# Weight conversions behind attention, ordered behind the newest split or copy

## The chip, the core and the metric

The kernel runs on one core of a Trainium2 chip: TensorE (PE in the profile, with its weight loads as PEld), VectorE (DVE), ScalarE (ACT), GpSimd (POOL) and SyncE (SP), each with a queue of its own that it works through in order. The metric is device time in microseconds of one execution, the median of the runs. 1 % is 10.4 us here.

## What is computed

Attention with a causal mask and a cumulative bias, then two dense layers with an activation between two matrix products each. Only the first dense layer (`_moe_ref`) lies in the stretch that the change touches; its four matrices are stored as 64-bit floats, which the kernel must turn into 32-bit pairs first.

```python
def _moe_ref(x, w_in, w_out):            # x: 2304 x 512, w_in: 512 x 2048, w_out: 2048 x 512
    h = x @ w_in
    g = h * (1.0 / (1.0 + np.exp(-1.702 * h)))
    return (g @ w_out).astype(np.float32)

def reference(**kwargs):
    ...
    attn_out = _attn_ref(**attn_kwargs)  # 4 batches, 8 heads, 576 positions, 64 wide
    B, H, S, D = attn_out.shape
    x = np.ascontiguousarray(attn_out.transpose(0, 2, 1, 3)).reshape(B * S, H * D)
    x = _moe_ref(x=x, **moe_kwargs)
    return _moe2_ref(x=x, **moe2_kwargs)
```

## The kernel before

**Precision and tiles.** Every operand of a matrix product is kept as a high and a low part, so that each product is three matmuls. A dense layer is cut into 16 columns of d_ff (`f`, 128 wide each); the weights of one `f` are a unit `u` of two halves, `w_in` and `w_out`, each 128 x 512. The tokens are cut into 8 blocks of 288.

**Stages of the first layer.** `mlp1_first` runs `f` = 0 to 4; for the first three batches it runs as filler within attention, for the last batch alone behind it, and each of its blocks ends in copies `st` of the sums (line 613, on ScalarE for odd `d`, on VectorE for even ones). `mlp1_rest` then runs `f` = 5 to 11 over all 8 blocks, and again `f` = 12 to 15. One step of it is `stage1` (12 matmuls into a bank `h`, line 575), `act1` (tanh on ScalarE, a product on VectorE, then the split of the result: the high part `gh` by ScalarE, line 589, the low part `gl` by VectorE, line 592) and `out1` for the step two before it (12 matmuls, line 599). At a block's end VectorE adds the block's sums to those of the pass before (`xp`, line 659), GpSimd's queue stores them and SyncE's queue loads the next block's (line 649). The second dense layer, `mlp2`, follows.

**Conversions.** `convert` (line 495 on) turns one half of raw 64-bit weights into a high and a low part: three ScalarE instructions (lines 500, 502, 508) and, behind attention, five on VectorE (503, 504, 505, 507, 509). Some halves go straight into a unit `u`; others into `park` and from there by GpSimd's queue into DRAM (line 555), to be fetched later. `task` puts a conversion in a queue; `emit` takes the next one, `look_ahead` keeps `LEAD` = 2 loads of raw weights (lines 489, 491, SyncE's queue) ahead of it; the raw tiles have 4 buffers. Behind attention `mlp1_first` emits eight conversions (`EARLY`), and `mlp1_rest` calls `tick` at each step, which by `PACE` = 0.5 emits one at every second step, 40 in all.

**What sets the order.** The program is written in the order above, but a scheduler orders each engine's queue by times that it reckons itself when the program is built; an instruction may stand well ahead of its place in the text when its inputs are reckoned to be there. `issue_after`, through `behind`, binds the instructions that a block of code emits to stand behind a given instruction of the same engine; it adds no wait on another engine. Within attention conversions are already bound in this way behind `self.tail` (the newest exponential and reciprocal); `wide` is false there and true behind it.

Of the kernel before, what the change touches and what calls it, by code (L numbers as in the profile page):

```python
# [15 lines left out]
AF = mybir.ActivationFunctionType  # L16
# [18 lines left out]
HB = S // 2  # L35
# [24 lines left out]
class Fused:  # L60
    def __init__(self, tc, q, k, v, s, w1i, w1o, w2i, w2o, a, b, out):
        self.tc, self.nc = tc, tc.nc
        self.q, self.k, self.v, self.s = q, k, v, s
        self.w = {n: (i.bitcast(I32), o.bitcast(I32)) for n, i, o in ((1, w1i, w1o), (2, w2i, w2o))}
        self.a, self.b, self.out = a, b, out
        self.units = {}
        self.acts = []


    def consts(self, pool):  # L70
# [456 lines left out]
    def emit(self, n):  # L527
        for _ in range(min(n, len(self.queue))):
            src, work = self.queue.pop(0)
            work(self.ahead.pop(0) if self.ahead else self.load_raw(src))  # L530
            self.look_ahead()

    def look_ahead(self):
# [49 lines left out]
    def act1(self, pool, h, w, bufs):  # L583
        nc = self.nc
        g = pool.tile([P, HB], F32, name="g", tag="g", bufs=2)
        nc.scalar.activation(g[:, :w], h, AF.Tanh, scale=0.851)  # L586
        nc.vector.scalar_tensor_tensor(g[:, :w], g[:, :w], 1.0, h, ALU.add, ALU.mult)  # L587
        gh = pool.tile([P, HB], F32R, name="gh", tag="gh", bufs=bufs)
        nc.scalar.activation(gh[:, :w], g[:, :w], AF.Copy)  # L589
        gl = pool.tile([P, HB], F32R, name="gl", tag="gl", bufs=bufs)  # L590
        eng = nc.vector if self.wide else nc.gpsimd
        gl_op = eng.tensor_tensor(gl[:, :w], g[:, :w], gh[:, :w].bitcast(F32), ALU.subtract)  # L592
        self.acts.append(gl_op)
        return gh, gl

    def out1(self, acc, u, d, g, first, last):
# [7 lines left out]
    def out1_block(self, pool, blk, gs):  # L604
        nc = self.nc
        for d in range(KD):
            acc = self.bank("a" if self.wide else "M", f"a{blk}_{d}")
            for f in range(F1):
                self.out1(acc[:, :HB], self.units[1, f], d, gs[f], f == 0, f == F1 - 1)
                if f % 2 and f < F1 - 1:  # L610
                    yield 0.74
            st = pool.tile([P, HB], F32, name="st", tag="st", bufs=2)
            (nc.scalar.copy if d % 2 else nc.vector.tensor_copy)(st, acc[:, :HB])
            nc.sync.dma_start(self.x2p[d * P : (d + 1) * P, blk * HB : (blk + 1) * HB], st)
            yield 0.37

# [328 lines left out]
```

## Time and profile before

| | us |
|---|---|
| median of 3 runs | 1044.78 |
| the runs | 1044.45, 1044.78, 1049.55 |
| the profiled execution | 1049.78 |
| its span, first to last instruction | 1048.0 |

The profiled execution lies 5.0 us above the median and next to the slowest of the three runs. A slice or window row gives each engine's busy time and, in brackets, its count of instructions in that stretch; PEclk is the granted share of TensorE's full clock; a timeline row gives start, duration, engine, line and, in square brackets, how long the engine stood idle just before and what released it. Attention ends at about 315 us, `mlp1_first` of the last batch at 347.9, `mlp1_rest` at 642.

### The profile page before, as it was taken

To read this page: it belongs to the slowest core of one execution; us is meant where nothing else is said; L and a number is where in the kernel's file an instruction comes from. 1 tells how busy PE (TensorE), PEld (TensorE's weight loads), DVE (VectorE), ACT (ScalarE), POOL (GpSimd) and SP (SyncE) were. 2 spreads that over 40 slices of the span, in tenths; PEclk is the share of its full clock that TensorE was granted. 3 is DMA by queue.
4 is the path that set the end of the run, shared out by engine and by line. 5 is a ranking of instruction groups with operands and counts; after the bars stand their busy time and mean duration, and the time that the engine had idled before them with its cause. 6 is when DMAs were issued, how large, how long until landed. Compare 5 with 4: busy or idle time off the path is not lost.

```text
span 1048.0 us, 19871 instructions
## 1 busy us (share of the span) xinstructions
PE 1015.2 (97%) x7074; PEld 945.2 (90%) x7074; DVE 812.1 (77%) x1874; ACT 721.3 (69%) x1660; POOL 322.7 (31%) x429
## 2 busy tenths in 40 slices
PE   7978999999999999989999999999999999999997
PEld 4767999999999999989999999899899999999996
DVE  6898868766637898885397345898998988989886
ACT  5898879888756765654264235787877777777775
POOL 6357745634320003331111112223222222222222
PEclk9998999999999999999999999999999999999999
DMA  7455356454217658894246537010010100100000
GB/s 180 119 155 147 99 150 192 121 138 101 54 41 278 193 173 287 280 302 150 71 145 206 179 121 259 1 31 31 1 61 1 31 31 1 59 3 1 31 1 31
DMA packets 79596, 116.72 MB, mean 111 GB/s; under 512 B 25697, under 2 KB 63585, under 8 KB 77901
## 3 DMA queue, kind: packets, MB, share of 16 engines
q1 hardware_dynamic: 73128, 95.96, 31.0%
q0 software_dynamic: 6144, 19.19, 5.1%
q8 instruction: 56, 0.92, 0.4%
q14 instruction: 44, 0.35, 0.1%
q10 hardware_dynamic: 224, 0.30, 0.1%
HBM read 75.08 MB, written 32.05 MB: 102 GB/s over the span
## 4 chain that ended last, share of the span: by engine, by line
PE 82%; ACT 4%; issue 4%; DMA 4%; DVE 3%; POOL 2%; SPq 0%; ACTq 0%; POOLq 0%; DVEq 0%
PE h L575 33%; PE a L751 19%; PE a L599 15%; PE s L255 5%; PE O L370 4%; PE tp L344 3%; DMA raw<-in_moe_w_in_dram 2%; POOL wd L555 1%; ACT bt L292 1%; PE idle L79 1%; DMA raw<-in_moe_w_out_dram 1%; PE tk L218 1%; DVE bt L285 1%; ACT kh L180 1%; PE tq L218 1%
## 5 line engine op out<-in xcount | busy, mean ns | idle before, releaser
L575 PE MATMUL h<-x,u 128*128 128x288 f32 x1536 | 231.2, 298 | 7.2 <-DVE g L587 4.2
L599 PE MATMUL a<-gh,u 128*128 128x288 f32 x1024 | 227.1, 297 | 2.2 <-ACT gh L589 2.2
L575 PEld LDWEIGHTS h<-x,u 128*128 128x128 f32 x1536 | 213.6, 189 | 10.6 <-DVE g L587 4.9
L734 POOL TENSOR_TENSOR gl<-u,gh 128x384 fp32r<-128x384 f32 x96 | 105.5, 1099 | 291.4 <-ACT gh L732 255.7
L599 PEld LDWEIGHTS a<-gh,u 128*128 128x128 f32 x1024 | 171.1, 188 | 4.1 <-ACT gh L589 2.6
L575 PE MATMUL h<-y,u 128*128 128x384 f32 x864 | 165.7, 336 | 0.0
L575 PEld LDWEIGHTS h<-y,u 128*128 128x128 f32 x864 | 152.9, 188 | 6.2
L599 PE MATMUL a<-gl,u 128*128 128x288 f32 x512 | 147.7, 295 | 0.8 <-DVE gl L592 0.7
L751 PE MATMUL a<-u,gh 128*128 128x512 f32 x432 | 114.6, 394 | 0.9 <-ACT gh L732 0.9
L304 POOL TENSOR_SCALAR bt<-bt,sm 128x128 f32<-128x128 f32 (+2 forms) x144 | 82.1, 582 | 105.8 <-DVE sm L301 66.4
L660 POOL DMA_DIRECT2D x<-xp x64 | 35.3, 552 | 226.6 <-DVE g L587 95.4
L586 ACT ACTIVATE g<-h 128x288 f32<-128x288 f32 x128 | 51.5, 406 | 75.0 <-PE h L575 67.0
L599 PEld LDWEIGHTS a<-gl,u 128*128 128x128 f32 x512 | 96.4, 188 | 2.3 <-DVE gl L592 1.8
L292 ACT ACTIVATE bt<-bt,mn 128x128 f32<-128x128 f32 (+2 forms) x144 | 83.6, 582 | 18.0 <-DVE mn L285 17.1
L751 PEld LDWEIGHTS a<-u,gh 128*128 128x128 f32 x432 | 80.0, 188 | 14.9 <-ACT gh L732 1.8
L587 DVE SCALAR_TENSOR_TENSOR g<-g,h 128x288 f32<-128x288 f32 x128 | 57.1, 449 | 45.8 <-ACT g L586 45.6
L285 DVE CUSTOM_DVE_ANT_0 bt<-s,mask 128x128 f32<-128x128 f32 (+2 forms) x144 | 69.0, 482 | 26.4 <-PE s L255 22.4
L732 ACT ACTIVATE gh<-u 128x384 fp32r<-128x384 f32 x96 | 50.6, 528 | 55.6 <-DVE u L730 55.4
L717 ACT ACTIVATE y<-h,cf 128x384 f32<-128x384 f32 x96 | 55.5, 579 | 36.7 <-PE h L575 36.7
L255 PE MATMUL s<-k 68*128 68x256 f32 (+2 forms) x192 | 72.1, 380 | 5.5 <-DMA k<-stgA 3.2
L722 DVE SCALAR_TENSOR_TENSOR y<-s,cf,y 128x384 f32<-128x384 f32 x96 | 59.3, 618 | 21.2 <-ACT s L719 19.5
L730 DVE SCALAR_TENSOR_TENSOR u<-y,u 128x384 f32<-128x384 f32 x96 | 73.6, 767 | 1.1
(107 smaller groups left out, 2068.0 us busy)
## 6 DMA issues: line engine op xcount, KB each, us to landing
raw<-in_moe_w_in_dram SPq DMA_DIRECT2D x24, 512.0 KB, 5.2
raw<-in_moe_w_out_dram SPq DMA_DIRECT2D x24, 512.0 KB, 3.8
x<-xp POOLq DMA_DIRECT2D x64, 144.0 KB, 2.8
wd<-park POOLq DMA_DIRECT2D x36, 256.0 KB, 5.0
u<-wd SPq DMA_DIRECT2D x8, 1024.0 KB, 10.4
x2p<-st SPq DMA_DIRECT2D x32, 144.0 KB, 2.4
xp<-x2p SPq DMA_DIRECT2D x32, 144.0 KB, 2.7
xp<-x SPq DMA_DIRECT2D x32, 144.0 KB, 2.7
```

Source lines behind the costliest of these rows:

```text
L255: nc.tensor.matmul(sc[: c1 - c0, :w], lhsT=q[:, c0:c1], rhs=k[:, j0 : j0 + w], start=m == 0, stop=m == 1,)
L285: nc.vector.tensor_tensor_reduce(bt[:, j0 : j0 + w], sc[:, :w], mask, 1.0, 3.0e38 if i == 0 else mn[:, 0:1], ALU.add, ALU.min, mn[:, i : i ...
L292: ex = nc.scalar.activation(bt[:, :n], bt[:, :n], AF.Exp, bias=mn[:, i : i + 1], scale=-1.0, accum_out=sm[:, col : col + 1],)
L304: nc.gpsimd.tensor_scalar(bt[:, :n], bt[:, :n], inv[:, i : i + 1], 1.0, ALU.mult, ALU.mult)
L575: nc.tensor.matmul(ps_tile, lhsT=u[:, wl, kk * P : (kk + 1) * P], rhs=x(xl, kk), start=(n == 0), stop=(n == 3 * KD - 1),)
L587: nc.vector.scalar_tensor_tensor(g[:, :w], g[:, :w], 1.0, h, ALU.add, ALU.mult)
L599: nc.tensor.matmul(acc, lhsT=u[:, wl, d * P : (d + 1) * P], rhs=g[gl], start=(first and i == 0), stop=(last and i == 2),)
L717: nc.scalar.activation(y, h, AF.Abs, scale=cf[:, 4:5])
L722: nc.vector.scalar_tensor_tensor(y, s, cf[:, 7:8], y, ALU.mult, ALU.add)
L730: last = nc.vector.scalar_tensor_tensor(p, y, 2.0, p, ALU.subtract, ALU.mult)
L734: nc.gpsimd.tensor_tensor(gl, p, gh.bitcast(F32), ALU.subtract)
L751: nc.tensor.matmul(accs[m], lhsT=g[gl][:, m * P : (m + 1) * P], rhs=u[:, wl, :], start=(f == 0 and i == 0), stop=(f == NF - 1 and i == 2),)
```

## The change

Three things are recorded where they are issued: the newest `gh` or ScalarE copy `st` under "act", and the newest `gl` or VectorE copy `st` under "dve". When a conversion's turn comes and `wide` is set, its instructions on these two engines are bound behind those. The load of the raw weights stays outside this, and runs two ahead as before. The list `acts`, which nothing read, goes.

```diff
-        self.acts = []
+        self.newest = {}
...
             src, work = self.queue.pop(0)
-            work(self.ahead.pop(0) if self.ahead else self.load_raw(src))
+            staged = self.ahead.pop(0) if self.ahead else self.load_raw(src)
+            with self.behind(self.newest.values() if self.wide else ()):
+                work(staged)
             self.look_ahead()
...
-        nc.scalar.activation(gh[:, :w], g[:, :w], AF.Copy)
+        self.newest["act"] = nc.scalar.activation(gh[:, :w], g[:, :w], AF.Copy)
...
-        self.acts.append(gl_op)
+        self.newest["dve"] = gl_op
...
-            (nc.scalar.copy if d % 2 else nc.vector.tensor_copy)(st, acc[:, :HB])
+            key, copy = ("act", nc.scalar.copy) if d % 2 else ("dve", nc.vector.tensor_copy)
+            self.newest[key] = copy(st, acc[:, :HB])
```

The queues that come of it are equal up to the end of `mlp1_first` and from `mlp2` on; between them all five differ. In the rows below `h2_2_8` is the `h` of block 2, `f` = 8; `raw` and `cvx` are a conversion's tiles, told apart by their last number; a line number behind 527 stands two or three higher after the change.

**ScalarE, block 2 of the first pass of `mlp1_rest`.** Before:

```order
L586 ACTIVATE g_6171<-h2_2_8_6158 128x288
L589 ACTIVATE gh_6134<-g_6131 128x288
L508 ACTIVATE park_5475<-cvx_6520 128x512
L500 ACTIVATE raw_6609<-raw_6609 128x512
L502 ACTIVATE cvx_6773<-raw_6609 128x512
L589 ACTIVATE gh_6174<-g_6171 128x288
L586 ACTIVATE g_6216<-h2_2_9_6203 128x288
L586 ACTIVATE g_6248<-h2_2_10_6235 128x288
L500 ACTIVATE raw_6698<-raw_6698 128x512
L589 ACTIVATE gh_6219<-g_6216 128x288
```

After, the same steps:

```order
L588 ACTIVATE g_6171<-h2_2_8_6158 128x288
L508 ACTIVATE park_5475<-cvx_6105 128x512
L591 ACTIVATE gh_6174<-g_6171 128x288
L500 ACTIVATE raw_6026<-raw_6026 128x512
L502 ACTIVATE cvx_6190<-raw_6026 128x512
L588 ACTIVATE g_6216<-h2_2_9_6203 128x288
L591 ACTIVATE gh_6219<-g_6216 128x288
L508 ACTIVATE park_5475<-cvx_6190 128x512
L588 ACTIVATE g_6248<-h2_2_10_6235 128x288
```

The 25th raw tile (`raw_6609`), whose conversion has its turn at block 4, stood ahead of `gh_6174` of block 2; now the 18th (`raw_6026`) stands there, behind that `gh`, and each split follows its tanh with at most one conversion instruction between them.

**ScalarE, the end of `mlp1_first`** (`a7_1`, `a7_3`: sums of the last block; `raw_5353`: the eighth raw tile). Before:

```order
L613 COPY st_5419<-a7_1_5403 128x288
L500 ACTIVATE raw_5353<-raw_5353 128x512
L502 ACTIVATE cvx_5429<-raw_5353 128x512
L508 ACTIVATE u1_10_5301<-cvx_5302 128x512
L508 ACTIVATE u1_10_5301<-cvx_5344 128x512
L613 COPY st_5466<-a7_3_5450 128x288
L500 ACTIVATE raw_5500<-raw_5500 128x512
```

After:

```order
L616 COPY st_5419<-a7_1_5403 128x288
L500 ACTIVATE raw_5353<-raw_5353 128x512
L502 ACTIVATE cvx_5429<-raw_5353 128x512
L508 ACTIVATE u1_10_5301<-cvx_5302 128x512
L616 COPY st_5466<-a7_3_5450 128x288
L508 ACTIVATE u1_10_5301<-cvx_5344 128x512
L588 ACTIVATE g_5489<-h2_0_5_5476 128x288
```

One of the two line-508 instructions moved behind the last copy; the eighth raw tile still stands ahead of it.

**VectorE, the end of block 6 of the first pass** (`a2_6_5_0` to `_3`: the block's four sums). Before:

```order
L587 SCALAR_TENSOR_TENSOR g_7489<-g_7489,h2_7_5_7476 128x288
L592 TENSOR_TENSOR gl_7494<-g_7489,gh_7492 128x288
L659 TENSOR_TENSOR xp_7315<-a2_6_5_0_7225,xp_7315 128x288
L587 SCALAR_TENSOR_TENSOR g_7536<-g_7536,h2_7_6_7523 128x288
L659 TENSOR_TENSOR xp_7317<-a2_6_5_1_7226,xp_7317 128x288
L659 TENSOR_TENSOR xp_7319<-a2_6_5_2_7227,xp_7319 128x288
L659 TENSOR_TENSOR xp_7321<-a2_6_5_3_7228,xp_7321 128x288
```

After:

```order
L594 TENSOR_TENSOR gl_7494<-g_7489,gh_7492 128x288
L503 TENSOR_SCALAR cvx_7512<-cvx_7512 128x512
L504 TENSOR_SCALAR cvx_7512<-cvx_7512 128x512
L662 TENSOR_TENSOR xp_7315<-a2_6_5_0_7225,xp_7315 128x288
L589 SCALAR_TENSOR_TENSOR g_7536<-g_7536,h2_7_6_7523 128x288
L505 SCALAR_TENSOR_TENSOR cvx_7512<-raw_7366,cvx_7512 128x512
L662 TENSOR_TENSOR xp_7317<-a2_6_5_1_7226,xp_7317 128x288
L662 TENSOR_TENSOR xp_7319<-a2_6_5_2_7227,xp_7319 128x288
L662 TENSOR_TENSOR xp_7321<-a2_6_5_3_7228,xp_7321 128x288
```

No conversion stood near this block's end before; now one lies around and between its four adds.

## Rows read from the trace of the kernel before

**Rows 1.** The page: span, busy times of the engines, granted clock in 40 slices.

```profile
span 1048.0 us, 19871 instructions
PE 1015.2 (97%) x7074; PEld 945.2 (90%) x7074; DVE 812.1 (77%) x1874; ACT 721.3 (69%) x1660; POOL 322.7 (31%) x429
PEclk9998999999999999999999999999999999999999
```

**Rows 2.** Windows by stage, all engines: from, to, length, busy times and counts.

```profile
core 0: us, PE busy (x) PEld busy (x) DVE busy (x) ACT busy (x) POOL busy (x), PEclk, DMA share, GB/s
325.00:350.00 25.00, 22.51 (x168) 22.02 (x166) 20.81 (x46) 17.42 (x36) 0.00 (x0) 1.00 0.76 243
350.00:404.00 54.00, 53.84 (x395) 53.84 (x396) 51.44 (x114) 37.24 (x78) 5.82 (x11) 0.97 0.64 195
404.00:475.00 71.00, 64.20 (x471) 62.34 (x471) 57.01 (x126) 39.45 (x84) 23.40 (x42) 1.00 0.88 288
475.00:525.00 50.00, 50.00 (x380) 50.00 (x379) 21.49 (x51) 17.11 (x40) 6.52 (x12) 1.00 0.34 108
525.00:575.00 50.00, 50.00 (x380) 50.00 (x379) 44.37 (x100) 29.32 (x62) 6.96 (x12) 1.00 0.51 170
```

**Rows 3.** TensorE's waits from 404 to 475: us in total, times, longest.

```profile
PE h L575 <- DVE g L587: 4.2, 3, 1.6
PE a L599 <- ACT gh L589: 2.2, 2, 1.4
```

**Rows 4.** Timeline of ScalarE and TensorE around 414 us.

```profile
413.76 0.65 ACT L500 ACTIVATE raw<-raw 128x512 int32<-128x512 uint32 x1 [3.65 <-DMA raw<-in_moe_w_in_dram]
...
414.87 0.43 ACT L589 ACTIVATE gh<-g 128x288 fp32r<-128x288 f32 x1
...
415.34 0.79 PE L599 MATMUL a<-gh,u 128*128 128x288 f32 x4 [1.43 <-ACT gh L589]
```

**Rows 5.** ScalarE's waits from 404 to 475, the two on raw weights.

```profile
ACT raw L500 <- DMA raw<-in_moe_w_out_dram: 12.6, 7, 4.4
ACT raw L500 <- DMA raw<-in_moe_w_in_dram: 11.6, 6, 3.7
```

**Rows 6.** Line 500's instructions from 350 to 404, 404 to 475, 475 to 642.

```profile
L500 ACT ACTIVATE raw<-raw x15: 666/684/702, 350.0 to 401.6; 128x512 int32<-128x512 uint32 x15
...
L500 ACT ACTIVATE raw<-raw x16: 652/676/702, 407.2 to 474.3; 128x512 int32<-128x512 uint32 x16
...
L500 ACT ACTIVATE raw<-raw x9: 667/683/695, 475.2 to 552.3; 128x512 int32<-128x512 uint32 x9
```

**Rows 7.** Timeline of ScalarE and TensorE where `mlp1_rest` begins.

```profile
346.88 0.67 ACT L500 ACTIVATE raw<-raw 128x512 int32<-128x512 uint32 x1 [1.98 <-DMA raw<-in_moe_w_out_dram]
...
349.19 0.63 ACT L508 ACTIVATE u<-cvx 128x512 fp32r<-128x512 f32 x1 [0.57 <-DVE cvx L507]
349.73 0.38 ACT L613 COPY st<-a 128x288 f32<-128x288 f32 x1
...
347.58 0.30 PE L599 MATMUL a<-gh,u 128*128 128x288 f32 x1
350.16 2.41 PE L575 MATMUL h<-x,u 128*128 128x288 f32 x12 [2.29 <-ACT st L613]
```

**Rows 8.** Windows of 2 us behind that wait; the column behind POOL is PEclk.

```profile
350.00:352.00 2.00, 1.84 (x11) 1.84 (x12) 2.00 (x6) 1.25 (x3) 0.00 (x0) 0.80 0.89 170
352.00:354.00 2.00, 2.00 (x10) 2.00 (x9) 2.00 (x4) 0.78 (x2) 0.00 (x0) 0.50 0.66 243
354.00:356.00 2.00, 2.00 (x15) 2.00 (x14) 1.65 (x5) 1.63 (x5) 0.00 (x0) 0.85 0.63 152
```

**Rows 9.** Timeline of VectorE and TensorE around a block's end without conversions.

```profile
592.44 1.18 DVE L659 TENSOR_TENSOR xp<-a,xp 128x288 f32<-128x288 f32 x3
...
595.94 0.46 DVE L592 TENSOR_TENSOR gl<-g,gh 128x288 fp32r<-128x288 f32 x1 [0.51 <-ACT gh L589]
...
594.67 0.29 PE L599 MATMUL a<-gh,u 128*128 128x288 f32 x1
...
600.67 0.29 PE L599 MATMUL a<-gh,u 128*128 128x288 f32 x1
```

**Rows 10.** Groups by line, 350 to 642: one of the conversion's five VectorE instructions.

```profile
L505 DVE SCALAR_TENSOR_TENSOR cvx<-raw,cvx 128x512 int32<-128x512 int32 x42 | 28.6, 682 | 0.0
```

**Rows 11.** Waits of SyncE's queue from 404 to 475: the longest in total.

```profile
SPq L489 <- DVE cvx L507: 22.0, 7, 4.8
```

## The prediction

> **What bounds the kernel now.** The page comes first: TensorE is busy for 1015.2 of 1048.0 us [rows 1], so nearly all the time is matmul and only its gaps and its slow clock can be won. Which gaps the change can reach follows from where the queues differ: from the end of `mlp1_first` to the beginning of `mlp2`, some 320 to 642 us. The second view is therefore the windows by stage over that stretch [rows 2]. They show one bad stage: from 404 to 475 TensorE is busy for 64.20 of 71 us and runs 471 matmuls, while from 475 to 575 it is never idle and runs 380 in each 50 us, one per 0.1316 us. In the bad stage the DMA engines are busy for 0.88 of the time.
>
> The third view is who makes TensorE wait there: the product on VectorE that frees a bank `h`, 4.2 us, and the high part `gh`, 2.2 us [rows 3]. Neither VectorE nor ScalarE is full (57.01 and 39.45 of 71 us, rows 2), so something stands ahead of these instructions in their queues. The timeline names it: at 413.76 ScalarE begins line 500 of a conversion after 3.65 us of idleness for a raw load, the `gh` queued behind it starts at 414.87, and TensorE, which wanted it, begins at 415.34 after 1.43 us [rows 4]. ScalarE loses 12.6 and 11.6 us in this stage to such loads, 13 times [rows 5]. So the stage is bound by the order of ScalarE's queue: conversions stand ahead of the splits although their data are not there. They stand there because they were put early: 15 + 16 of the 40 in `mlp1_rest` run before 475 us and only 9 after it [rows 6], though `PACE` gives them one turn in every second step to about step 80 of 88.
>
> **What the change does, part by part.**
>
> *The title's loads* change nothing by themselves: `LEAD` is 2 on both sides. What moves is SyncE's queue: a conversion now takes its raw tile, and frees the buffer of the load four later, nearer its turn, so loads spread as well.
>
> *Nothing is added or removed* on an engine: the same eight instructions per conversion, the same DMAs, no wait on another engine. Matmul time stays.
>
> *The stalls of 404 to 475.* In the order after, each `gh` has at most one conversion instruction between it and its tanh, and a conversion's line 500 stands behind the `gh` of its turn. Two loads ahead are four steps ahead, 4 x 24 matmuls x 0.1316 = 12.6 us by the rate of rows 2. The longest wait for a load was 4.4 us [rows 5], with the loads queued late; with 12.6 us of lead it should be gone. The load on the DMA engines falls too. The stage held 471 / 24 = 19.6 steps and 16 conversions, 0.82 per step; at 0.5 per step the share of 0.88 becomes about 0.88 x 0.5 / 0.82 = 0.54, which is near the 0.51 of 525 to 575, where TensorE never waited [rows 2]. What goes is bounded from below by the idle time, 71 - 64.20 = 6.8 us, and from above by the matmuls that are short, 71 - 471 x 0.1316 = 9.0 us (some may only be missing from the trace). I take the middle, 7.9 us.
>
> *The start of `mlp1_rest`.* TensorE's last matmul of `mlp1_first` starts at 347.58 and the next stage at 350.16, held by the last copy `st` [rows 7]. Ahead of that copy stood line 500 on the eighth raw tile, which waited 1.98 us for its load, and two line-508 instructions, the second of which waited 0.57 us for VectorE. Now one of them stands behind the copy: the copy follows line 500, 502 and one 508, about 1.65 us after the load instead of 2.85 (349.73 - 346.88), so 1.2 us are won if the load lands as before. That load should be issued earlier as well, since in SyncE's queue one store of a copy no longer stands ahead of it. The floor is a copy that starts when the matmul ends, near 347.9, and leaves about 0.7 of the 2.29 us. So 1.1 to 1.6; I take 1.3.
>
> *The clock behind it.* Behind that wait the granted clock was 0.80, 0.50 and 0.85 in three windows of 2 us [rows 8], which costs 0.4 + 1.0 + 0.3 = 1.7 us; 0.50 is the 1.2 GHz level. The waits in the bad stage, at most 1.6 us [rows 3], left it at 1.00 [rows 2]. The wait that remains here is about 1 us and so nearest to those: I take the whole 1.7 us, with 0 as the other end. The Trainium skill says (TensorE: Matmul & The Clock Gate, Part 1) that the throttled state is the default, that activity releases it, and that how many slow matmuls a start gets varies from run to run; by the rule the 1.7 us may also stay, and the sum would then be 8.2 instead of 9.9.
>
> *What is new.* From 475 us on VectorE and ScalarE carry conversions where they carried few. VectorE's 21.49 of 50 us rises towards the 44.37 of 525 to 575, where TensorE ran at its full rate [rows 2], so the load alone costs nothing. At a block's end a conversion now lies between the adds. In a block's end without one the last three adds, from 592.44, were done at 593.62 and the first matmul that needs a freed bank came at 594.67, those for the last sum still later [rows 9]; a line 505 of 0.68 us [rows 10] fits into 1.05 us, two more of such size ahead of the first add would not quite. A `gl` done at 596.40 is used in the third `out1` from there, at 600.67 [rows 9], so a split has 4.3 us of cover. I put 1 us on all this, between 0 and 3. What is late next, once the stalls are gone, is TensorE itself.
>
> *Queues.* SyncE's loads of `xp` wait for stores and stand between raw loads; the 12.6 us of lead cover such a wait. GpSimd's queue only issues stores here; a parked half's stores now come at a conversion's turn, so fewer `xp` stores stand behind them.
>
> **The sum.** -7.9 - 1.3 - 1.7 + 1.0 = -9.9 us, against the profiled execution of 1049.78: 1039.9. That execution lies 5.0 us above the median of 1044.78. If its extra time lies outside this stretch, the median becomes 1034.9; if it lies in the stalls that go, 1039.9. The slices below full clock lie in the first 105 us [rows 1], before the change acts, and such dips are the nearest known thing that may differ between executions; so I stay close to the first and say 1036.
>
> **The rivals.**
>
> *The buffers bind, not the order: nearly no change.* SyncE's queue waited 22.0 us of the bad stage for VectorE to release raw tiles [rows 11], and there are 4 of them on both sides. If the pace of buffers sets the stalls, the loads stay late, the waits only move along the stage, and the boundary alone is won: 1044.8 - 1.3 = 1043.5. Against it: from 525 to 575 conversions run through the same 4 tiles with VectorE at 44.37 of 50 us and TensorE never idle, and half a conversion per step asks for less than 0.82. The Trainium skill (Perfetto Trace Analysis, Identifying Performance Opportunities) takes consistent bubbles on the engine that should be full as a sign that memory for the next tile may be short; by that rule the result is this rival's.
>
> *Every conversion now stands where it can hurt: slower.* Before, 9 conversions ran after 475 us without harm. Now all 40 lie among the splits, with VectorE's line 503 right behind a `gl` and ahead of adds and products. If the real loads land later than the builder reckons, by more than the 4.3 us of cover, each costs what one cost in the bad stage, at most 9.0 / 16 = 0.56 us. All 40 then cost 22.5 us, 14.6 more than the 7.9 now: 1059. Against it: the DMA share falls, and a load has 12.6 us.
>
> *The change doesn't do what it says* is out: in the queues each conversion of `mlp1_rest` does stand behind the split of its turn.
>
> **How the numbers follow.** The forecast gets 0.72, with its own range from 1031 (upper stall bound 9.0, the run's extra outside, nothing new, some small gaps more) to 1040 (the extra inside). The buffers' rival gets 0.22, the slower one 0.06. The range goes from 1031 to 1043, which takes in most of the second case and leaves out the slower one. A measurement can tell about 0.5 % from no change, 5.2 us: faster means below 1039.6. From the same cases: faster 0.72, within 0.5 % 0.22, slower 0.06.
>
> **What would show it.** Right: TensorE never idle by more than a few tenths between 352 and 642, its rate 380 matmuls per 50 us all along, no `ACT raw <- DMA` wait above 1 us there, line 500 spread to about 600 us, DMA share under 0.65. Of the boundary: a wait near 1 us and a clock of 1.00 behind it. Wrong: the waits of rows 3 turn up again at a later place, or at blocks' ends behind the adds; or the raw loads are issued late by SyncE, so that line 500 waits as before.

## The result, and the profile after

| | before | after |
|---|---|---|
| median of 5 runs, us | 1044.78 | 1037.0 |
| lowest and highest | 1042.91, 1049.55 | 1035.24, 1038.33 |
| the profiled execution | 1049.78 | 1037.67 |
| its span | 1048.0 | 1035.9 |

The ratio of the runs is 0.9918, with a 95 % interval of 0.9891 to 0.9945: faster by 8.6 us, or 5.7 to 11.4. The time of 1037.0 lies 1.0 above the 1036 that was forecast and within 1031 to 1043. A kernel that is built to the same five queues (`e1_act_only`, below) gave 0.9898 in another comparison, which is 10.7 us.

The first view is again the page of after. The span is 12.1 us shorter, and TensorE (PE) is busy for 3.7 us less with the same 7074 instructions; the others have the same counts too [rows 1].

```profile
span 1035.9 us, 19876 instructions
PE 1011.5 (98%) x7074; PEld 944.2 (91%) x7074; DVE 818.9 (79%) x1874; ACT 724.8 (70%) x1660; POOL 321.8 (31%) x429
```

The windows by stage of after, with the columns of [rows 2]: from, to, length, busy time and count of PE, PEld, DVE, ACT and POOL, then PEclk, DMA share and GB/s.

```profile
350.00:404.00 54.00, 54.00 (x410) 54.00 (x409) 44.83 (x96) 32.00 (x67) 5.67 (x10) 1.00 0.51 157
404.00:475.00 71.00, 71.00 (x538) 71.00 (x537) 53.31 (x114) 37.70 (x78) 18.53 (x34) 1.00 0.67 220
475.00:525.00 50.00, 50.00 (x380) 50.00 (x379) 37.08 (x79) 26.77 (x55) 10.95 (x20) 1.00 0.68 229
525.00:575.00 50.00, 50.00 (x380) 50.00 (x379) 40.27 (x88) 26.64 (x56) 9.10 (x16) 1.00 0.65 213
```

The bad stage is gone: 71.00 of 71 us busy with 538 matmuls, where it was 64.20 and 471 [rows 2]. From 350 to 404 the clock is 1.00 where it was 0.97. VectorE's work is level now, between 0.74 and 0.83 of each stage, where it swung between 0.43 and 0.95.

TensorE's waits from 340 to 645 us in after, in the form of [rows 3] (us in total, times, longest), come down to one:

```profile
PE h L577 <- ACT st L616: 1.1, 1, 1.1
```

And ScalarE's waits for raw weights from 350 to 642, in the form of [rows 5]: 46.2 us in 30 waits before, this one after.

```profile
ACT raw L500 <- DMA raw<-in_moe_w_out_dram: 0.6, 1, 0.6
```

The timeline of after around 414 us, beside [rows 4], shows the same spot at work. Line 500 stands behind the split now, and does not wait:

```profile
413.93 0.41 ACT L588 ACTIVATE g<-h 128x288 f32<-128x288 f32 x1 [1.81 <-PE h L577]
414.23 0.62 ACT L508 ACTIVATE park<-cvx 128x512 fp32r<-128x512 f32 x1
414.86 0.45 ACT L591 ACTIVATE gh<-g 128x288 fp32r<-128x288 f32 x1
415.21 0.67 ACT L500 ACTIVATE raw<-raw 128x512 int32<-128x512 uint32 x1
415.25 1.76 PE L577 MATMUL h<-x,u 128*128 128x288 f32 x12
```

The 1.81 us in brackets is ScalarE waiting for TensorE, which is how it should be in a stage that TensorE bounds.

**Where the 12.1 us of the spans went.** The last matmul of `mlp1_first` ends at 347.05 (347.58 before): 0.5. From there to the first of `mlp1_rest` it is 1.44 us where it was 2.58 [rows 7]: 1.1. `mlp1_rest`, from that matmul to its end, takes 281.2 us (348.49 to 629.66) where it took 291.6: 10.4. Before had seven gaps of TensorE over 0.25 us in it, 7.9 us in all between 413 and 471; after has none. The half clock at its start cost 1.7 us [rows 8]; after shows 1.00 there. That makes 9.6 of the 10.4; the other 0.8 lies in steps from one matmul to the next that are longer than usual by less than 0.25 us each.

### The profile page after: what moved, and what is told of

It reads as the page before. It is cut to its first block, busy times and chain, and to the rows that moved or that the text cites. A ratio compares the mean times of both kernels' runs of the same rounds, so it can differ in the third digit from the quotient of the medians.

```text
span 1035.9 us, 19876 instructions
## 1 busy us (share of the span) xinstructions
PE 1011.5 (98%) x7074; PEld 944.2 (91%) x7074; DVE 818.9 (79%) x1874; ACT 724.8 (70%) x1660; POOL 321.8 (31%) x429
## 4 chain that ended last, share of the span: by engine, by line
PE 89%; ACT 3%; DMA 3%; DVE 2%; POOL 1%; issue 1%; SPq 0%; ACTq 0%; DVEq 0%; POOLq 0%
PE h L577 37%; PE a L754 19%; PE a L601 19%; PE s L255 5%; PE O L370 5%; PE tp L344 3%; DMA raw<-in_moe_w_in_dram 1%; ACT bt L292 1%; DMA stgA<-in_moe_w_in_dram 1%; DMA x2p<-st 1%; PE tq L218 0%; PE tp L323 0%; PE tk L218 0%; DVE sm L300 0%; ACT kh L180 0%
## 5 line engine op out<-in xcount | busy, mean ns | idle before, releaser
L601 PE MATMUL a<-gh,u 128*128 128x288 f32 x1024 | 231.7, 297 | 0.0
L601 PE MATMUL a<-gl,u 128*128 128x288 f32 x512 | 149.9, 294 | 0.2 <-DVE gl L594 0.2
L285 DVE CUSTOM_DVE_ANT_0 bt<-s,mask 128x128 f32<-128x128 f32 (+2 forms) x144 | 69.1, 482 | 28.9 <-PE s L255 24.8
L591 ACT ACTIVATE gh<-g 128x288 fp32r<-128x288 f32 x128 | 56.4, 442 | 41.9 <-DVE g L589 40.2
L725 DVE SCALAR_TENSOR_TENSOR y<-s,cf,y 128x384 f32<-128x384 f32 x96 | 59.3, 618 | 20.5 <-ACT s L722 19.3
```

Source lines behind the costliest of these rows:

```text
L285: nc.vector.tensor_tensor_reduce(bt[:, j0 : j0 + w], sc[:, :w], mask, 1.0, 3.0e38 if i == 0 else mn[:, 0:1], ALU.add, ALU.min, mn[:, i : i ...
L591: self.newest["act"] = nc.scalar.activation(gh[:, :w], g[:, :w], AF.Copy)
L601: nc.tensor.matmul(acc, lhsT=u[:, wl, d * P : (d + 1) * P], rhs=g[gl], start=(first and i == 0), stop=(last and i == 2),)
L725: nc.vector.scalar_tensor_tensor(y, s, cf[:, 7:8], y, ALU.mult, ALU.add)
```

## The experiments

One question stood behind the result: the change does four things at once, and any of them could have removed the stalls. **The buffers**: raw tiles come free at another pace. **A, the spread**: conversions run evenly to about 600 us instead of being crowded before 475. **B, the count**: fewer splits have a line 500 between tanh and `gh` in ScalarE's queue (30 of 88 before, 1 after, counted in the built queues). **E, the traffic**: the DMA engines have less to do at a time, so loads land sooner. And **D, the reckoning**: an unbound line 500 is placed where the scheduler reckons its load to land; the load lands later on the chip, and all that stands behind it on ScalarE waits. Bound behind the split of its turn, it finds its data there. (The scheduler's reckoned times are in no trace, so that half of D can only be argued; where line 500 stands behind its load can be measured.) Ratios below are to the kernel before on the same chip, with 95 % intervals. Two of the experiments add transfers and change no result; no other leaves out or adds any computation.

**Fewer raw tiles.** If buffers set the stalls, three instead of four must hurt in both kernels. In before, and the same edit in after:

```diff
-            raw = self.stg.tile([P, 512, 2], I32, name="raw", tag="raw", bufs=4)
+            raw = self.stg.tile([P, 512, 2], I32, name="raw", tag="raw", bufs=3)
...
-                    st = self.stg.tile([P, 512, 2], I32, name="ost", tag="raw", bufs=4)
+                    st = self.stg.tile([P, 512, 2], I32, name="ost", tag="raw", bufs=3)
```

> The kernel before with 3 buffers for raw weights instead of 4; line 500 then stands between tanh and gh in 26 splits instead of 30. Buffers bind: the stalls grow by a third or more, ratio 1.003 or above. Theory A: a conversion waits for its load in either case and the queue holds about as many of them ahead of a split, ratio 0.999 to 1.003, ScalarE's wait on raw loads 40 to 65 us.

> The changed kernel with 3 buffers for raw weights instead of 4. Theory A: at one conversion in two steps (6.3 us) three tiles still give each load over 6 us, more than the 4 us that a load takes: no waits on raw loads in mlp1_rest, ratio 0.992 to 0.993; at the start of mlp1_rest, where eight conversions follow each other closely, up to 2 us may be lost. The rival of the prediction (buffers bind): waits on raw loads of 10 us and more, ratio 0.996 or above.

Before with three tiles: 1.0004 [0.9986, 1.0021]. After with three tiles: 0.994 [0.9924, 0.9956]. The window 404 to 475 of before with three tiles:

```profile
404.00:475.00 71.00, 66.44 (x489) 64.70 (x488) 60.89 (x135) 41.03 (x87) 24.41 (x44) 1.00 0.89 293
```

And the same window of after with three tiles:

```profile
404.00:475.00 71.00, 71.00 (x539) 71.00 (x538) 52.93 (x112) 37.72 (x79) 18.59 (x34) 1.00 0.68 220
```

With a buffer less the order of after still keeps TensorE full, and the order of before still stalls, no worse than with four: its gaps behind 352 us come to 7.7 us against 7.9, a part of them now behind 475. So the buffers' rival is out within `mlp1_rest`. SyncE's waits for raw tiles point the same way. In after they still stand there from 404 to 475, 37.9 us beside a TensorE that never idles, so the 22.0 of [rows 11] were no sign of a bound:

```profile
SPq L489 <- DVE cvx L507: 21.4, 5, 6.4
SPq L491 <- DVE cvx L507: 16.5, 5, 6.4
```

What after loses with three tiles it loses at the start of `mlp1_rest`, where the eighth raw tile comes late: TensorE's wait there in after with three tiles.

```profile
PE h L577 <- ACT st L616: 3.0, 1, 3.0
```

Its window from 350 us on, behind that wait, with a clock of 0.95:

```profile
350.00:404.00 54.00, 54.00 (x391) 54.00 (x391) 42.96 (x94) 29.85 (x63) 4.61 (x8) 0.95 0.46 141
```

**More traffic.** Every half that is parked behind attention is stored a second time, into memory that nothing reads. In after (`e9`) and in before (`e10`):

```diff
+            self.second = self.dram.tile([P, 4, 512], F32, name=f"we{layer}_{f}")
...
+            if self.wide:
+                eng.dma_start(self.second[:, half + 2 * i], buf[:, i].bitcast(F32))
```

> The changed kernel with every store of a parked half made twice, the second into memory that nothing reads: the DMA share of 404 to 475 us goes from 0.67 to near that of the bad stage before, 0.88. Theory D (an unbound line 500 stands where the builder reckons its load to land and the chip lands it later; bound behind a split, a load has some 20 us): loads may take half as long again and nobody waits, ScalarE's waits on raw loads in mlp1_rest stay below 3 us, TensorE stays full, ratio 0.991 to 0.994. Theory E (the gain is the lighter DMA traffic of the spread conversions): the stalls come back in part, ratio 0.995 to 0.999.

> The same doubled stores in the kernel before. A line 500 stands between tanh and gh in 28 splits there. Theory D: the loads land later still than the builder reckons and ScalarE waits longer each time, 60 to 90 us in all against 50, ratio 1.003 to 1.012. If the length of the loads didn't matter, ratio 1.000 and waits as before.

After with the stores twice: 0.9895 [0.9875, 0.9915]. Its windows:

```profile
404.00:475.00 71.00, 71.00 (x538) 71.00 (x537) 53.09 (x113) 37.68 (x78) 30.76 (x56) 1.00 0.88 304
475.00:525.00 50.00, 50.00 (x380) 50.00 (x379) 37.25 (x78) 26.32 (x56) 17.58 (x32) 1.00 0.83 282
```

The DMA share is the 0.88 of the bad stage [rows 2], and TensorE never idles. So E is out: lighter traffic is not what the change gives. Before with the stores twice came out a little faster than before, 0.9959 [0.9933, 0.9985], where a slower run was expected; that expectation missed. ScalarE waits for raw weights 31 times there (53.5 us from 350 to 645), more than before's 46.2, yet TensorE's gaps come to 4.4 us instead of 7.9. The added stores made the scheduler reckon anew and the queues differ, so this run tells only that ScalarE's waiting is no measure of what TensorE loses.

**The two halves of the binding.** Each engine's binding alone. `e1` keeps ScalarE's:

```diff
-            with self.behind(self.newest.values() if self.wide else ()):
+            with self.behind([self.newest["act"]] if self.wide else ()):
```

> Only the binding on ScalarE is kept, the one on VectorE left out. All five queues come out the same, row by row, as with both. So the time is that of the changed kernel: ratio 0.990 to 0.994, no wait of ScalarE on raw loads above 1 us. If the binding on VectorE mattered by itself, this would be slower, but there is no place in the queues where it could show.

`e2` keeps VectorE's:

```diff
-            with self.behind(self.newest.values() if self.wide else ()):
+            with self.behind([self.newest["dve"]] if self.wide else ()):
```

> Only the binding on VectorE is kept; ScalarE's conversion instructions are free again. In the queues the 40 conversions of mlp1_rest then stand spread over steps 7 to 80, as after the change, but in 11 of 88 splits a line 500 stands between the tanh and its gh (30 before, 1 after the change). Theory A (before, conversions chased their loads as fast as raw buffers came free, so that a line 500 nearly always waited; spreading them ends that): loads are early, ScalarE waits on raw loads below 5 us in all, TensorE loses under 1 us in the bad stage, ratio to before 0.992 to 0.993. Theory B (the place of line 500 ahead of a gh costs time whatever the pace): 11/30 of the 8 us come back, ratio about 0.995.

`e1` is built to the same queues as after, row for row on all five, and gave 0.9898 [0.9874, 0.9921]: VectorE's binding adds nothing, since its part of a conversion needs ScalarE's. `e2` gave 1.0083 [1.0066, 1.0101], slower than before. It spreads the conversions to the end of the stage and its DMA share is low, and still TensorE is short in both of these windows:

```profile
404.00:475.00 71.00, 67.40 (x495) 65.61 (x495) 47.04 (x99) 32.77 (x69) 15.89 (x29) 1.00 0.58 190
475.00:525.00 50.00, 45.48 (x332) 44.00 (x331) 33.34 (x71) 23.80 (x51) 11.60 (x22) 1.00 0.61 195
```

ScalarE's waits in `e2` from 320 to 650 us:

```profile
ACT raw L500 <- DMA raw<-in_moe_w_out_dram: 37.6, 22, 4.1
ACT raw L500 <- DMA raw<-in_moe_w_in_dram: 28.6, 19, 2.8
```

So A alone does not do it, and with a DMA share of 0.58 heavy traffic is not what makes these loads late either. B falls as well: only 11 splits have a line 500 in between here, against 30 before, and the time is longer. The loss takes a longer way. The timeline of `e2` at 475 us:

```profile
474.15 0.66 ACT L500 ACTIVATE raw<-raw 128x512 int32<-128x512 uint32 x1 [2.83 <-DMA raw<-in_moe_w_out_dram]
...
475.26 0.39 ACT L588 ACTIVATE g<-h 128x288 f32<-128x288 f32 x1
475.69 0.46 DVE L589 SCALAR_TENSOR_TENSOR g<-g,h 128x288 f32<-128x288 f32 x1 [1.98 <-ACT g L588]
...
476.66 1.18 DVE L662 TENSOR_TENSOR xp<-a,xp 128x288 f32<-128x288 f32 x3
...
477.17 0.40 PE L601 MATMUL a<-gh,u 128*128 128x288 f32 x1 [1.62 <-DVE xp L662]
```

Line 500 waits 2.83 us for its load, the tanh behind it is late, VectorE's product waits 1.98 us for that tanh, and behind the product stand the adds that free a sum's bank, for which TensorE waits 1.62 us. One late load goes through two in-order queues.

How far line 500 stands behind its own load can be worked out from the trace: for each conversion of `mlp1_rest`, the start of line 500 minus SyncE's issue of that tile's load. The median of 40 is 4.9 us in before, 4.0 in `e2` and 20.5 in after. When a load lands can be had from its semaphore, which is updated 16 times per load. In before 35 of the 40 line-500 instructions start within 0.2 us of their load's landing, in `e2` all 40, in after one. A load itself takes 3.4 to 8.5 us in after, 3.9 in the median; of those issued from 404 to 475 the median is 4.2 us in after and in `e2`, and 5.9 in before. So unbound, line 500 starts as its load lands, whether loads are slow as in before or not as in `e2`. That is the measured half of D's picture.

**Double pace.** After with two turns where it had one:

```diff
-PACE = 0.5
+PACE = 1.0
```

> The changed kernel with PACE = 1.0: a conversion has its turn at every step, bound behind the newest split as in the change. Theory A: conversions outrun their loads again wherever the turn comes faster than a load and its buffer, so ScalarE waits on raw loads by over 15 us and TensorE gets back half to all of the stalls of before: ratio 0.996 to 1.000. Theory C (being bound behind the split is enough, the pace doesn't matter): TensorE loses under 1 us, ratio 0.992.

0.9933 [0.9916, 0.995], faster than was expected. Bound conversions at double pace wait again, 15 times and 28.2 us from 350 to 645, and TensorE loses 3.0 us in three gaps:

```profile
404.00:475.00 71.00, 68.51 (x512) 67.66 (x511) 54.52 (x122) 37.38 (x81) 22.56 (x40) 1.00 0.84 279
```

The median from a load's issue to its line 500 falls to 6.0 us. So A is half right: the binding needs a pace at which four tiles give a load time to land.

**Every second conversion bound.** Up to here D rested on comparing kernels whose orders differ in much. This run has both kinds in one execution, at the same pace, in the same traffic.

```diff
-            with self.behind(self.newest.values() if self.wide else ()):
+            self.turn = getattr(self, "turn", 0) + 1
+            with self.behind(self.newest.values() if self.wide and self.turn % 2 else ()):
```

> The kernel after with every second conversion bound, the others free as before; all 40 still lie at one per second step or up to three steps early, and 10 of the 88 splits have a free line 500 between tanh and gh. If an unbound line 500 is put where its load is reckoned to land and really lands later (the theory so far), the two kinds differ within one run: from load issue to line 500 some 4 to 6 us for the free ones and over 12 us for the bound ones; ScalarE waits for raw loads 10 to 22 times, 15 to 35 us, nearly all at free ones; TensorE loses 1 to 5 us between 350 and 645; ratio to before 0.992 to 1.000. If the even spreading alone is what helps (the rival), ScalarE waits under 5 us, TensorE's gaps there come to under 0.5 us and the ratio is that of after, 0.989 to 0.993.

The two kinds come apart wholly. From issue to line 500 the 20 bound ones take 9.9 to 24.8 us (median 21.4), the 20 free ones 3.8 to 7.4 (median 5.5). The free ones are the loads of `w_out`, and ScalarE waits for 19 of those 20 and for none of the bound ones, which are the loads of `w_in`. The kind of weight is not what divides them: in after the `w_out` loads are bound too, their median is 20.5 us, and ScalarE waits for one of the 20, 0.6 us. Its only row on raw weights from 350 to 645:

```profile
ACT raw L500 <- DMA raw<-in_moe_w_out_dram: 51.6, 19, 5.1
```

The timeline of this kernel at 454 to 458 us (its lines are one higher than after's) has one of each, the free one at 455.94 and a bound one at 457.75:

```profile
449.92 0.33 SPq L491 DMA_DIRECT2D raw<-in_moe_w_out_dram  x1
...
455.94 0.65 ACT L500 ACTIVATE raw<-raw 128x512 int32<-128x512 uint32 x1 [5.12 <-DMA raw<-in_moe_w_out_dram]
456.49 0.39 ACT L589 ACTIVATE g<-h 128x288 f32<-128x288 f32 x1
456.78 0.43 ACT L592 ACTIVATE gh<-g 128x288 fp32r<-128x288 f32 x1
...
457.27 1.33 PE L602 MATMUL a<-gh,u 128*128 128x288 f32 x4 [2.81 <-ACT gh L592]
...
457.75 0.67 ACT L500 ACTIVATE raw<-raw 128x512 int32<-128x512 uint32 x1
```

The spread alone, which would have given after's time, is refuted: the ratio is 1.0044 [1.0025, 1.0064], slower than before. In size D's expectation missed too: it said 15 to 35 us of waiting, 1 to 5 us lost and 0.992 to 1.000; it was 51.6, 10.6 and 1.0044. So the place of a free line 500 is shown to be the cause of its wait, why the scheduler puts it there is argued, and what a wait costs TensorE is not settled. Per us that ScalarE waits for raw weights from 350 to 645, TensorE's gaps are 0.17 us in before (7.9 of 46.2), 0.23 in `e2` (13.9 of 59.6), 0.21 here (10.6 of 51.6), 0.08 in `e10` (4.4 of 53.5) and 0.11 in `e4` (3.0 of 28.2). It depends on what stands behind the waiting instruction, which differs in each.

**The boundary.** Two runs on the start of `mlp1_rest`. In `e5` the copies `st` are no longer recorded, so that conversions bind behind `gh` and `gl` alone:

```diff
-            self.newest[key] = copy(st, acc[:, :HB])
+            copy(st, acc[:, :HB])
```

> The kernel after without the two records of the copies st: conversions behind attention are bound behind the newest gh and gl alone. The queues differ from after at the end of mlp1_first only: line 500 and 502 of the eighth raw tile stand ahead of the last but one ScalarE copy again. By the prediction's step for the boundary (what stands ahead of the copies sets the wait) the wait at the start of mlp1_rest grows from 1.1 to 1.5 to 2.5 us, and half the clock for some 3 us behind it (1.7 us) may come back, as it stood behind the waits of 2.19 us and more so far; ratio 0.990 to 0.995. If the copies' records are of no use, the wait stays at 1.0 to 1.2 us, the clock at 1.00 and the ratio at 0.989 to 0.993. Either way no wait of ScalarE for raw loads above 1 us and no gap of TensorE over 0.25 us between 352 and 640 us.

In `e11` the eighth conversion of `mlp1_first` is emitted behind its loop instead of in it:

```diff
-EARLY = tuple(range(3, 40, 5))
+EARLY = tuple(range(3, 35, 5))
...
+                    K.emit(1)
```

> The changed kernel with the eighth conversion of mlp1_first emitted behind its last copy, so that in ScalarE's queue no raw tile stands ahead of that copy but those of the conversions before. If the remaining wait of 1.1 us at the start of mlp1_rest is line 500 on the eighth raw tile, it falls to about 0.7 us or less; if it is the matmul's end and the copy itself, it stays at 1.0 to 1.1. The total moves by less than the measurement tells: ratio 0.990 to 0.994.

`e5`: 0.9908 [0.9879, 0.9937]; TensorE's wait at the boundary in `e5`:

```profile
PE h L577 <- ACT st L616: 1.8, 1, 1.8
```

`e11`: 0.9909 [0.9887, 0.9931]. The same wait in `e11`:

```profile
PE h L577 <- ACT st L616: 1.0, 1, 1.0
```

Recording the copies takes 0.7 us from that wait in this pair of profiles, which the times of the runs can't show; `e9`, with the same order here as after, waits 1.5, so a part of the 0.7 may be scatter. What after still waits is no matter of the eighth tile: with its conversion out of the way 1.0 us is left. The timeline of after says what that is:

```profile
346.16 0.32 SPq L617 DMA_DIRECT2D x2p<-st  x1
347.05 0.30 PE L601 MATMUL a<-gh,u 128*128 128x288 f32 x1
347.19 0.62 ACT L508 ACTIVATE u<-cvx 128x512 fp32r<-128x512 f32 x1
348.03 0.40 ACT L616 COPY st<-a 128x288 f32<-128x288 f32 x1 [0.23 <-DMA x2p<-st]
348.49 1.71 PE L577 MATMUL h<-x,u 128*128 128x288 f32 x11 [1.14 <-ACT st L616]
```

The last matmul is done at 347.35 and line 508 at 347.81, but the copy begins only at 348.03, when a store has landed. There are two `st` tiles, so the last ScalarE copy needs the tile of the ScalarE copy before it, whose store SyncE issued at 346.16; its semaphore has its 16th update at 347.94. The rest of the wait is the copy itself. In `e11`, with one line 508 alone between the two copies, the store shows plainly:

```profile
348.54 0.32 SPq L617 DMA_DIRECT2D x2p<-st  x1
350.42 0.40 ACT L616 COPY st<-a 128x288 f32<-128x288 f32 x1 [0.88 <-DMA x2p<-st]
```

In `e5` the last copy waits 1.39 us for the same store, since line 500 and 502 of the eighth tile stand ahead of the copy before it. So a part of the wait that is left hangs on the two `st` tiles: 0.22 us in after, behind line 508, and 0.5 in `e11`, behind the last matmul. A third tile was not tried. None of the ten beat after by more than the intervals are wide.

## Why the prediction was right, by its own steps

**What bounds the kernel** was read rightly: conversions stood ahead of the splits in ScalarE's queue although their data were not there. `e12` shows it for each conversion apart; `e1` and `e2` show that ScalarE's queue is where it has to be mended.

**The stalls, -7.9.** Right: the seven gaps over 0.25 us of before add up to 7.9, and none is left.

**The start of `mlp1_rest`, -1.3.** Right within 0.2: the gap between the two matmuls went from 2.58 to 1.44. The path was right only in part. The step had the copy follow line 500, 502 and one 508; in after these are done at 347.81, and what the copy still waits for, to 348.03, is the store that frees its `st` tile, which the step did not have. Its floor of about 0.7 us does not come out of [rows 7] either: from the copy's start to the first matmul it is 0.43 us there, so a copy that starts at 347.9 would leave some 0.45.

**The clock, -1.7.** Right, all of it: 1.00 from 350 us on, as it is in `e5`, `e1`, `e9`, `e10` and `e11`. The rule of the Trainium skill that stood behind this step (TensorE: Matmul & The Clock Gate, Part 1), by which the 1.7 us might have stayed, did not come to bear here.

**What is new, +1.0.** Did not come: TensorE has no gap over 0.25 us behind 348.49, at blocks' ends neither. This is the mis-sized term that made most of the sum's error for the profiled pair. The sum said 9.9, the stretch from the end of `mlp1_first` shows 11.5 (10.4 + 1.1). Of the 1.6 between them this term is 1.0, the steps longer by less than 0.25 us are 0.8, which no term held, and the boundary gave 0.2 less.

**The lead of a load** was put at four steps, 12.6 us; it is 20.5. The error lies in counting from the load's turn in the text. SyncE's load is bound to nothing and goes as soon as a raw tile is free, so the four buffers set the lead and not `LEAD`: built with `LEAD` = 0, all five queues are the same. The conclusion held, since more lead was found than was needed.

**The DMA share** was to fall to 0.54, under 0.65. It is 0.67, 0.68 and 0.65. The step scaled the share by conversions per step, but it is a share of time, and the steps go faster now: SyncE issues 11 raw loads from 404 to 475 where it issued 16, which by itself makes about 0.6. The step also took all traffic to follow the conversions; the blocks' sums, 12 loads and 12 stores in that window before and after, do not. It did no harm: `e9` runs at 0.88.

**Profiled run and median.** The text chose between 1034.9 (the extra 5.0 us of the profiled execution outside the stretch) and 1039.9 (inside it). The result lies between, at 1037.0. Nearly all 12.1 us between the two profiles lie at or behind the end of `mlp1_first` (0.5 ahead of it), and the two medians are 7.8 apart; that speaks for the extra being inside. Two profiles can't show it. In this comparison before scatters more, 6.6 us over 5 runs against 3.1 in after. That the forecast came within 1.0 us is in part luck: the sum was 1.6 too small for the profiles, and the choice of 1036, close to the first value, took more off the median than came off it (8.8 us against 7.8); the two misses partly offset each other.

**The rivals.** The buffers: out, by the runs with three tiles. The rule of the Trainium skill named there (Perfetto Trace Analysis, Identifying Performance Opportunities), by which bubbles point to memory for the next tile, would have sent a reader the wrong way in `mlp1_rest`, and the right way only at the boundary, where three raw tiles make the wait 3.0 us and where the two `st` tiles hold the last copy. "Every conversion now stands where it can hurt" did not happen to after, but its mechanism is real: it is what `e2` does, 1.0083, with 36 waits from 350 us on at loads that land after the turn of their line 500 has come. What decided was that after's loads have 20.5 us and `e2`'s 4.0.

## What to carry to other kernels

An instruction that waits for a transfer, in a queue that the bounding engine depends on, should be placed by what must go ahead of it and not by when its data are reckoned to arrive: behind the newest link of the chain it cost nothing here, and the buffers turned into lead for the load. Read such a stall from the idle time ahead of the waiting instruction and from what is queued behind it, through every queue that it reaches; neither the waiting engine's total, nor its busy share, nor the DMA share told here what it costs. A test that has both kinds in one execution (here: every second one bound) tells cause from company better than kernels that differ as a whole.

## What the runs showed of the hardware that was not expected

**The clock behind a gap.** These are TensorE's gaps of over 1.6 us from 330 to 645 us in all twelve profiles (after, `e1` and `e11` have none), less the usual step from one matmul to the next. At the start of `mlp1_rest`: 1.71 us (`e12`), 1.72 (`e9`), 1.75 (`e10`) and 1.96 (`e5`) were followed by 1.00; 2.19 (`e2`), 2.46 (before), 3.22 (`e8`) and 3.36 (`e3`) by half the clock, 1.2 GHz, for a few us. Later in the stage: 1.72 (`e4`) and 1.78 (before, `e2`) by 1.00; 2.26 and 2.96 (both `e12`) by half; but 2.27 (`e10`) by 1.00. So the length of the gap alone does not decide. The 2-us windows of `e10` around its gap from 488.30 to 490.70, with the columns of [rows 8]:

```profile
488.00:490.00 2.00, 0.59 (x5) 0.36 (x3) 1.33 (x3) 1.39 (x4) 0.94 (x2) 1.00 0.67 221
490.00:492.00 2.00, 1.29 (x10) 1.33 (x11) 2.00 (x7) 1.71 (x4) 1.46 (x4) 1.00 0.81 285
492.00:494.00 2.00, 2.00 (x17) 2.00 (x17) 2.00 (x5) 0.52 (x2) 1.82 (x4) 1.00 0.92 321
```

And the 2-us windows of `e12` behind its gap from 454.17 to 457.27:

```profile
456.00:458.00 2.00, 0.73 (x3) 0.73 (x4) 0.94 (x3) 1.81 (x5) 0.00 (x0) 0.70 0.96 344
458.00:460.00 2.00, 2.00 (x10) 2.00 (x10) 1.29 (x4) 1.85 (x4) 0.00 (x0) 0.50 0.60 176
```

**Transfers under load.** Here are the loads of raw weights, 512 KB each, that were issued from 404 to 475 us, from SyncE's issue to the 16th update of the load's semaphore. The median was 4.2 us in after (11 loads, 3.6 to 5.6, DMA share 0.67), 4.8 in `e9` (12 loads, 3.8 to 6.6, share 0.88), 5.9 in before (16 loads, 3.7 to 8.7, share 0.88) and 6.6 in `e10` (12 loads, 3.6 to 8.8, share 0.93). At the same share before's loads took 1.1 us longer than `e9`'s; why was not tried, and so few loads don't show whether something beside the share decides. The profile's own row on time to landing is no substitute: for `w_in` in before, from 352 to 645, it rests on 4 of 19 loads.
